# Other row counts for the split weight transfers of a fused attention and spectral-mixing kernel

## The chip, the cores and the metric

The kernel runs on one core of one Trainium2 chip. Times are device microseconds of one execution; lower is better. A profile of one execution of the kernel before, with the records of its instructions, semaphores and DMA packets, is at hand.

## The reference

Two parts follow each other. The first is attention over 8 batches, 8 heads, 576 positions and 64 channels a head. The first four heads see the last 32 positions, the other four see the positions whose distance is a multiple of 32. The second part takes the joined heads as x (8 x 576 x 512), transforms along the positions, keeps 64 modes, multiplies each mode's 512 channels by that mode's own complex 512 x 512 matrix, transforms back, adds x, and adds a rectified product with one more 512 x 512 matrix:

```python
X = np.fft.rfft(x, axis=1)
Xr, Xi = (np.real(X[:, :n_modes]), np.imag(X[:, :n_modes]))
Yr = np.einsum('bmd,mde->bme', Xr, w_r) - np.einsum('bmd,mde->bme', Xi, w_i)
Yi = np.einsum('bmd,mde->bme', Xr, w_i) + np.einsum('bmd,mde->bme', Xi, w_r)
Y[:, :n_modes] = Yr + 1j * Yi
y = np.fft.irfft(Y, n=S, axis=1)
u = x + y
return (u + np.maximum(u @ w_ch, 0.0)).astype(np.float32)
```

The matrices w_r and w_i, 64 x 512 x 512 float32 each, are by far the largest inputs: 134 MB of the 163 MB that are read.

## The kernel before, in words

The weights are streamed once, in half precision in the core's memory (the transfer converts them). A unit of the stream is a mode of one half of the 512 input channels: 128 units, in an order written out by hand in `ORDER`. Units 0 to 55 are half 1, modes 0 to 55; units 56 to 103 are half 0, modes 0 to 47; units 104 to 111 are half 1, modes 56 to 63; the rest is half 0, modes 48 to 63. Half 1 can start as soon as the strided heads are transformed, while the local heads are still being computed.

Units are fetched by `w_fetch` in pairs (two modes) or, for the pairs in `QUADS` between 13 and 53, in fours. One fetch has two transfers: the real parts go to partitions 0 to 63, the imaginary parts to partitions 64 to 127. Each partition receives, of each mode, one row of 2048 elements (8 KB read, 4096 bytes written). All of these transfers are issued by GpSimd (POOL), on one DMA queue. The last two pairs are fetched mode by mode. A fetch takes place in a ring of five pairs (`wring`); three early pairs use memory that is taken for something else later. `free_pairs` counts the pairs of the ring that the products have released: `mode_pair` (line 599) and `mode` (line 642) call `w_fetch` after the matmuls that read a pair, so each fetch waits on PE.

The table `UNEVEN` says for which units the real parts go out as several transfers of fewer rows, one behind the other, in place of one of 64 rows:

```python
if i in UNEVEN and not ri:
    a = 0
    for n in UNEVEN[i]:
        nc.gpsimd.dma_start(dst[a : a + n], rows[a : a + n])
        a += n
```

The key is the first unit of the fetch. Line 185 is the issue in this loop, line 188 that of a whole transfer, line 192 that of a single mode at the end. The bytes, the places that they are written to and the products that read them are the same however a transfer is cut; only the DMA engines that carry the rows can differ.

The order of the other work is by hand too. The strided heads of the eight batches come first (lines 262 to 394), then the local heads (lines 415 to 506), each followed by its forward transform (`dft`, line 534). From there on PE alternates between the products of the stream and the rest; a list of costs (`work`, `load`) in the third stage spreads the transposes and products with the last matrix over the fetches. Attention inputs are loaded in between by the same queue: strided ones as 64 rows and 8 rows, local ones as 128 rows. After the last products the inverse transform of the last modes, the rectified part and the output follow (lines 997 to 1122, 1141 to 1143); the output is stored by SyncE (SP).

Other transfers on the same 16 DMA engines are those of the output and constants, and the fetch of the engines' own instructions (queues 8 and 14 of the page).

Of the kernel before, what the change touches and what calls it, by code (L numbers as in the profile page):

```python
# [56 lines left out]
def kernel(  # L57
# [89 lines left out]
    SPLIT1, SPLIT0 = 56, 48  # L147
    ORDER = [(1, m) for m in range(SPLIT1)] + [(0, m) for m in range(SPLIT0)]
    ORDER += [(1, m) for m in range(SPLIT1, NM)] + [(0, m) for m in range(SPLIT0, NM)]
    UNEVEN = {64: (25, 12, 27), 84: (6, 54, 4), 94: (10, 54)}  # L150
    QUADS = {p for p in range(13, 54) if (p - 13) % 5 in (0, 2)}
    wring = pw.tile([128, 2 * NWBUF, 4, DM], F16, tag="w", bufs=1, name="wring")
    w_tiles = []
# [5 lines left out]
    def w_fetch(n=1):  # L159
        free_pairs[0] += n  # L160
        while len(w_tiles) < 2 * NM:
# [13 lines left out]
            for ri, src in enumerate((moe_w_r, moe_w_i)):  # L175
# [4 lines left out]
                if ri and not m:  # L180
                    dst, rows = dst[:, 1:nm], rows[:, 1:nm]
# [4 lines that stand above are left out]
# [1021 lines left out]
```

## Time and profile before

| | |
|---|---|
| median of 3 runs | 423.68 us (423.58 to 424.56) |
| the profiled execution's own time | 423.73 us |
| its span, first to last instruction | 421.7 us |
| granted TensorE clock, mean | 0.916 |
| busy: PE, PEld | 327.8 us, 201.8 us |
| busy: DVE, ACT, POOL | 236.9 us, 220.8 us, 112.2 us |
| moved by DMA | 91.62 MB written by 29914 packets |
| read from HBM | 162.83 MB |

The span is what the page and the trace count from; the time of an execution has 2.0 us around it. Times of a line are read from groups such as "L188 POOL DMA_DIRECT2D": a line of the kernel, the engine, the operation, what is written from what, how often, the busy time, the mean of one, and the idle time of the engine ahead of it with what ended it. In the chain of waits the last instruction is followed back to what released it. A DMA there stands from its issue to its landing.

A transfer lands when each of the 16 DMA engines has counted up its semaphore; the trace records the sixteen times, not which engine each belongs to. It also records start, length and size of every DMA packet, again without the engine.

### The profile page before, as it was taken

What the parts mean: (1) busy time and instruction counts of PE and PEld (TensorE: products, weight loads), DVE (VectorE), ACT (ScalarE), POOL (GpSimd) and SP (SyncE); (2) the same over time, 40 slices, a digit from 0 to 9 for tenths busy, and PEclk for the clock granted to TensorE, in tenths of its full rate; (3) what the DMA queues carried; (4) which work ended last, traced back from release to release, by engine and by line L of the source; (5) the groups of instructions that cost most, each with busy time, mean ns of one, the idle gap of its engine ahead of it and who ended that gap; (6) DMA issues with size and microseconds to landing.
All of it is one profiled execution on the core that took longest, in us unless ns stands there. A gap on an engine that the chain in (4) does not pass through costs nothing.

```text
span 421.7 us, 9817 instructions
## 1 busy us (share of the span) xinstructions
PE 327.8 (78%) x4156; PEld 201.8 (48%) x4156; DVE 236.9 (56%) x501; ACT 220.8 (52%) x423; POOL 112.2 (27%) x183
## 2 busy tenths in 40 slices
PE   3987878679999198888867858587569748889993
PEld 3866767564656155556534424244235423444320
DVE  3788788950364224555323627756276454665795
ACT  2687778742666157475752513532153345544693
POOL 8332333322422011212031211212112213220594
PEclk9999899956999779899995989999689988999998
DMA  8999999999999999999999999999999999999498
GB/s 149 211 211 212 214 212 213 210 212 210 215 213 213 214 214 214 214 215 214 212 214 214 213 214 214 214 213 213 213 213 215 213 214 214 213 213 182 177 380 341
DMA packets 29914, 91.62 MB, mean 217 GB/s; under 512 B 3952, under 2 KB 4720, under 8 KB 29872
## 3 DMA queue, kind: packets, MB, share of 16 engines
q0 software_dynamic: 24624, 81.28, 97.2%
q1 hardware_dynamic: 4816, 9.65, 6.2%
q8 instruction: 32, 0.52, 0.5%
q10 hardware_dynamic: 432, 0.08, 0.1%
q14 instruction: 10, 0.08, 0.0%
HBM read 162.83 MB, written 9.44 MB: 409 GB/s over the span
## 4 chain that ended last, share of the span: by engine, by line
DMA 48%; PE 27%; DVE 12%; ACT 6%; issue 4%; POOL 1%; DVEq 0%; POOLq 0%; ACTq 0%
DMA wring<-in_moe_w_i_dram 43%; PE y L599 6%; DMA wring<-in_moe_w_r_dram 4%; DVE xb L243 3%; DVE kz L285 3%; PE p L1032 2%; PE sc L534 2%; ACT X L253 2%; PE p L1052 2%; PE sc L461 1%; PE tp L415 1%; ACT PL L491 1%; PE y L534 1%; DVE rec L242 1%; DMA ring<-in_v_dram 1%
## 5 line engine op out<-in xcount | busy, mean ns | idle before, releaser
L599 PE MATMUL y<-wring,X 128*32 128x512 f16 (+1 forms) x424 | 49.1, 454 | 34.5 <-DMA wring<-in_moe_w_i_dram 34.5
L188 POOL DMA_DIRECT2D wring<-in_moe_w_r_dram x39 | 23.7, 607 | 186.4 <-PE y L599 162.5
L253 ACT ACTIVATE yr<-y 128x512 f16<-128x512 f32 x28 | 16.7, 597 | 59.7 <-PE y L599 58.0
L599 PEld LDWEIGHTS <-X 128*32 128x32 f16 (+1 forms) x448 | 21.9, 143 | 48.2 <-DMA wring<-in_moe_w_i_dram 33.0
L751 DVE COPY xo<-tp 128x512 f16<-128x512 f16 x32 | 22.1, 692 | 38.0 <-PE tp L749 38.0
L741 PE MATMUL sc<-w_cp,xT 128*128 128x512 f16 x128 | 37.4, 416 | 1.4 <-DVE xT L709 1.4
L750 ACT ACTIVATE v<-sc 128x512 f16<-128x512 f32 x32 | 19.1, 597 | 36.1 <-PE sc L741 36.1
L243 DVE TENSOR_TENSOR xb<-av,rec 90x256 f16<-90x256 f32 (+2 forms) x80 | 36.0, 450 | 2.7
L491 ACT ACTIVATE PL<-sc 128x480 f16<-128x480 f32 (+1 forms) x48 | 26.9, 578 | 17.2 <-PE sc L477 16.8
L242 DVE RECIPROCAL rec<-av 90x4 f32<-90x4 f32 (+2 forms) x80 | 14.6, 183 | 35.0 <-PE av L506 24.3
L422 DVE COPY qT<-tp 128x576 f16<-128x576 f16 x16 | 11.9, 752 | 37.3 <-PE tp L415 37.3
L1004 DVE TENSOR_TENSOR xo<-p,xo 128x512 f16<-128x512 f32 x32 | 20.6, 686 | 18.2 <-PE p L784 18.2
L188 POOL DMA_DIRECT2D wring<-in_moe_w_i_dram x42 | 25.5, 608 | 9.6 <-DMA wring<-in_moe_w_i_dram 5.3
L380 ACT ACTIVATE PL<-sc 90x360 f16<-90x360 f32 (+1 forms) x48 | 22.8, 490 | 7.0 <-PE sc L373 6.4
L253 ACT ACTIVATE v<-p 128x512 f16<-128x512 f32 x32 | 17.5, 594 | 14.9 <-PE p L784 14.8
L415 PE MATMUL tp<-cI_s,ring 64*64 64x64 f16 x864 | 23.1, 199 | 2.3 <-DVE qT L422 1.7
L253 ACT ACTIVATE v<-tp 128x640 f16<-128x640 f16 (+1 forms) x24 | 19.0, 807 | 10.6 <-PE tp L449 7.9
L461 PE MATMUL sc<-cMl_s,cI_s 128*128 128x480 f16 (+1 forms) x48 | 19.3, 403 | 5.0 <-ACT PL L491 3.4
L415 PEld LDWEIGHTS <-ring 64*64 64x64 f16 x864 | 18.3, 113 | 8.3 <-issue 4.2
L253 ACT ACTIVATE kz<-tp 64x360 f16<-64x360 f16 (+1 forms) x32 | 18.9, 592 | 6.1 <-PE tp L415 5.2
L1090 POOL TENSOR_TENSOR rl<-rl,xo 128x512 f32<-128x512 f32 x15 | 17.1, 1161 | 14.7 <-DVE rl L1083 13.0
L534 PEld LDWEIGHTS <-xb 108*128 108x128 f16 (+2 forms) x176 | 15.4, 106 | 10.8 <-DVE xb L243 6.2
(153 smaller groups left out, 763.1 us busy)
## 6 DMA issues: line engine op xcount, KB each, us to landing
wring<-in_moe_w_r_dram POOLq DMA_DIRECT2D x17, 1024.0 KB, 17.5
wring<-in_moe_w_i_dram POOLq DMA_DIRECT2D x16, 1024.0 KB, 21.8
wring<-in_moe_w_i_dram POOLq DMA_DIRECT2D x24, 512.0 KB, 17.8
wring<-in_moe_w_r_dram POOLq DMA_DIRECT2D x22, 512.0 KB, 14.7
out_dram<-osb SPq DMA_DIRECT2D x18, 256.0 KB, 2.4
out_dram<-osb SPq DMA_DIRECT2D x9, 512.0 KB, 3.3
ring<-in_v_dram POOLq DMA_DIRECT2D x8, 288.0 KB, 13.3
ring<-in_q_dram POOLq DMA_DIRECT2D x8, 288.0 KB, 13.5
```

The source lines that it names most:

```text
L188: nc.gpsimd.dma_start(dst, rows)
L243: nc.vector.tensor_tensor(out=dst, in0=val.rearrange("p h (q c) -> p h c q", c=4), in1=rec[0:n, 0:pieces] .to_broadcast((n, pieces, 64)) . ...
L253: nc.scalar.activation(out=out, in_=in_, func=ACTF.Copy)
L380: nc.scalar.activation(out=PS[0:n, ds(POFF[t], 4 * n)], in_=scp[0:n, 0 : 4 * n], func=ACTF.Exp, scale=SCALE,)
L415: nc.tensor.transpose(tp[ds(64 * hp, 64), ds(64 * i, 64)], qn[ds(64 * hp, 64), ds(64 * (9 * g + i), 64)], idn[ds(64 * hp, 64), ds(64 * hp, ...
L461: nc.tensor.matmul(scp[:, 0 : n * times].rearrange("p (h x) -> p h x", h=times), idn, mask_rows("cMl", n, times), start=True, stop=False,)
L491: nc.scalar.activation(out=dst, in_=src, func=ACTF.Exp, scale=SCALE)
L534: nc.tensor.matmul(xp[:, ds(192 * cp, 192)].rearrange("p (f m) -> p f m", f=3), xb[b][0:n, base + t, ds(128 * cp, 128)], F[0:n, :, t, :], ...
L599: nc.tensor.matmul(yp[ds(a, 32), :], Xh[half][pr, c].rearrange("p b r (h m) -> p (b r h) m", h=2)[:, :, mm % 32], wt[pr, XC[c], :], start= ...
L741: nc.tensor.matmul(vp, xT[:, ch], w_chs["cp"][:, ch, :], start=(ch == 0), stop=(ch == 3),)
L751: nc.vector.tensor_copy(out=xo.rearrange("p (h q c) -> p h q c", h=2, c=4), in_=tp[:, 0:512].rearrange("p (h c q) -> p h q c", h=2, c=4),)
L1004: nc.vector.tensor_tensor(out=xo[:, j], in0=up[j], in1=xo[:, j], op=AluOp.add)
```

## The change

Three fetches lose their cuts and four others are cut:

```diff
-    UNEVEN = {64: (25, 12, 27), 84: (6, 54, 4), 94: (10, 54)}
+    UNEVEN = {44: (20, 44), 64: (28, 36), 70: (50, 14), 86: (52, 12)}
```

Unit 44 is pair 22 (half 1, modes 44 and 45), unit 64 is pair 32 (half 0, modes 8 and 9); both are fetches of two modes. Units 70 and 86 are pairs 35 and 43, fetches of four modes, so each of their rows is twice as long in all. Unit 84 is pair 42, unit 94 pair 47; their real parts become single transfers of 64 rows. Eight pieces remain eight pieces, of four transfers in place of three. POOL issues one transfer fewer in all. No instruction of PE, DVE, ACT or SP is added, removed or moved.

## The prediction

> **What bounds the kernel now.** I read the page first, then the chain of waits, then the table of stretches for the last microseconds of the weight stream, then the trace's own records of DMA packets and landings. The page:
>
> ```profile
> span 421.7 us, 9817 instructions
> ...
> DMA  8999999999999999999999999999999999999498
> GB/s 149 211 211 212 214 212 213 210 212 210 215 213 213 214 214 214 214 215 214 212 214 214 213 214 214 214 213 213 213 213 215 213 214 214 213 213 182 177 380 341
> ...
> q0 software_dynamic: 24624, 81.28, 97.2%
> ...
> q8 instruction: 32, 0.52, 0.5%
> ...
> DMA 48%; PE 27%; DVE 12%; ACT 6%; issue 4%; POOL 1%; DVEq 0%; POOLq 0%; ACTq 0%
> ```
>
> From the second slice to the 36th the DMA engines never rest and move 210 to 215 GB/s. Sixteen engines at 213.5 GB/s write a packet of 4096 bytes each in 16 x 4096 / 213.5 = 0.307 us; in the packet records one engine's packets follow each other every 0.3045 us. So the stream of POOL's queue (q0) is a fixed amount of work, and its end can move only by how that work is shared out. The chain of waits around that end:
>
> ```profile
> 361.25 19.41 DMA wring<-in_moe_w_i_dram
> 380.66 0.28 issue
> 380.94 9.58 DMA wring<-in_moe_w_i_dram
> 390.52 0.14 issue
> 390.66 0.41 PE y L642 x8
> ```
>
> The last transfer lands at 390.52 us; PE's last mode starts 0.14 us later, and 31 us of output work follow. The stretches before it (PE, PEld, DVE, ACT, POOL busy, clock, then DMA share and GB/s):
>
> ```profile
> 384.00:385.00 1.00, 1.00 (x20) 0.69 (x19) 0.67 (x2) 0.77 (x2) 0.00 (x0) 1.00 1.07 217
> 385.00:386.00 1.00, 1.00 (x6) 0.47 (x5) 0.62 (x2) 0.54 (x2) 0.00 (x0) 1.00 1.00 197
> 386.00:387.00 1.00, 1.00 (x21) 0.65 (x21) 0.89 (x2) 0.55 (x2) 0.00 (x0) 1.00 0.91 180
> 387.00:388.00 1.00, 0.54 (x4) 0.05 (x4) 1.00 (x3) 0.60 (x1) 0.00 (x0) 1.00 0.91 180
> 388.00:389.00 1.00, 0.89 (x18) 0.68 (x19) 0.46 (x1) 0.00 (x0) 0.00 (x0) 1.00 0.68 135
> 389.00:390.00 1.00, 1.00 (x5) 0.29 (x3) 0.00 (x0) 0.00 (x0) 0.00 (x0) 1.00 0.29 57
> ```
>
> The engines do not finish together: the share falls from 1.07 to 0.29 over five microseconds. The sixteen landings of the last transfer say the same: first 385.44, last 390.52, mean 389.03. Perfect sharing would end the stream 1.49 us sooner; that is the most that any new split can gain. More than a few microseconds can be lost.
>
> **How a piece is shared out.** The page's 24624 packets tell. Data: 16256 rows of weights, 1728 of strided and 3072 of local attention inputs, 512 of w_ch, together 21568; one semaphore packet for each engine of 155 transfers is 2480. 576 are left over, 4 bytes long in the records. They are what an engine without rows gets in place of rows, if R rows go to the largest number of engines up to 16 that divides R, evenly: 25 rows to five (the other eleven get 10 each, 110), 12 to twelve (8), 27 to nine (42), 6 to six (20), 54 to nine (84, twice), 4 to four (24), 10 to ten (12), and the twelve 8-row inputs 16 each (192): 576 exactly. The Trainium skill ("DMA: Bandwidth & Descriptors", section on why a DMA increments its semaphore by 16) has this rule, and beside it an exception by which some transfers from GpSimd use rows/16, rounded up, per engine; that would leave 320 packets over, so the trace bears out the rule and not the exception. I also take it that each uneven piece starts at the engine after the last one of the piece before: with that, landing times modelled for 28 transfers from 230 to 385 us are off by 0.27 us on average, with a common start by 0.86. Call the engine where the first uneven piece starts place 0.
>
> **The change, per place.** Packets more (+) or fewer than an even share, counted from the row numbers; a row is two packets in a pair and four in a four-mode transfer. The third column is how far behind the mean of 16 each place lands the last transfer now, by the fit; braces mean that the order inside is not shown.
>
> ```
> place   old   new   lag now (us)                     difference      lag then
> 0       +2    +8    -2.03                            +6  +1.83       -0.20
> 1, 2    +6    +8    } {-1.16, -0.11, -0.10, +1.49}   +2  +0.61       see text
> 3       +6    +10   }  for places 1 to 4             +4  +1.22       see text
> 4       +6    -2    }                                -8  -2.44       see text
> 5, 6    -2    -6    } {+1.21, +1.47, +1.48}          -4  -1.22       at most +0.26
> 9       -2    -10   }  for places 5, 6, 9            -8  -2.44       about -1.0
> 7, 8    +8    +6    {+0.15, +0.38}                   -2  -0.61       at most -0.23
> 10..14  -6    -6    {-0.91, -0.27, +0.48, +0.73, +0.80}  0           at most +0.80
> 15      -6    +8    -3.60                            +14 +4.26       +0.66
> ```
>
> Why the spread exists at all: q8 fetches 32 blocks of 16 KB (0.5% of 16 x 421.7 us is 34 us, 1.05 us each), and the landing lists show these going round eight engines only, so those eight fall 1 us behind at every turn. The fit puts 5, 6 and 9 and five of 10 to 15 among them. The sixth of that group is the engine at -3.60. It is one of 13 to 15, since its third small piece of pair 42 lands 0.16 us after the second (278.02 after 277.86): too soon for two packets. I take 15: then the served engines (5, 6 and 9 to 14) and the unserved (15 to 4, and 7, 8) both come in neighbouring pairs; with 13 or 14 a pair would be broken.
>
> The four of places 1 to 4 include the engine at +1.49, one of those that end the stream. Four places are open to it. I lean to 4, and no more than lean: the eight go round in order of place, so the first fetch of the trace (same turn as the 17th, just ahead of 5) is on 13; counted from there 4 closes the first half of the sixteen, and the odd engine of a half is likelier at its border. The Trainium skill (same page, "Latency and other measured facts") calls engines 7 and 15 usually the slow ones; counted from 13, place 4 is number 7, and by that page the sum would be the one below with certainty. No row here shows an engine's number.
>
> With the slow one in place 4 it falls to 1.49 - 2.44 = -0.95. Place 3 then goes to +0.06 or +1.11, by which of three it is; 10 to 14 stay at +0.80. The last landing is 0.80 to 1.11 behind the mean, not 1.49: a gain of 0.69 or 0.38. I take 0.6, nearer the first.
>
> **The small terms.** One transfer fewer (154): about 0.02 us of semaphore packets per engine. Fillers: 192 + 24 + 40 + 8 + 24 + 120 + 8 + 48 + 16 = 480, 96 fewer, at 6 ns over 16 engines 0.04 us. POOL issues:
>
> ```profile
> L188 POOL DMA_DIRECT2D wring<-in_moe_w_r_dram x39 | 23.7, 607 | 186.4 <-PE y L599 162.5
> ```
>
> The extra issue before w_i at four places delays it and what POOL has queued behind (the next fetch and, near pair 35, the memsets of line 944) by 0.6 us; three old places give back five issues. This is hidden: POOL sits idle 186 us before this group alone, and each issue comes about 9 us ahead of its first packet (pair 22's first is issued at 168.85, and the engine furthest ahead lands it at 180.85). Without that cover it would cost 0.6 us once. Midway (250 to 294 us) places 5 and 6 run 6 packets over and the last landings come perhaps 1.6 us later than now; in exchange the 9 us spread after pair 42 goes. PE waits for weights either side and the end is set by the last transfer, so both cost nothing unless the queue runs dry, which 8 us of queued work prevent.
>
> PE must follow. Between 381 and 390 it is nearly full; before the last mode it idles 0.6 us, before the one at 388.11 another 0.57. So about 1.2 us can be taken over, then PE binds. 0.6 fits.
>
> The sum: 423.73 (the profiled execution; span 421.7, and 2 us around it) - 0.6 - 0.05 = 423.1. The median 423.68 is 0.05 lower, so 423.0 to 423.1.
>
> **Rivals.** First, the slow engine is in place 1 or 2: it lands 1.49 + 0.61 = 2.10 behind, 0.6 later than now, 424.3; in place 3, 2.71 behind, 424.9. For: the rows leave four places. Against: only the lean above.
>
> Second, and slower: the engine at -3.60 is not in place 15. Then 15 is a served engine, at -0.91 to +0.80, and +4.26 makes it the last by far: 3.35 to 5.06 behind, the stream 1.9 to 3.6 us longer, 425.6 to 427.3. It decides as soon as place 15 now lags more than 1.49 - 4.26 = -2.77. For: only 10 to 12 are excluded by a row. Against: the pairs.
>
> Third, the pieces are not laid as I say but from a fixed engine with rounded-up shares. Engines 0 to 3 would have 8 packets over now and 12 then, 4 x 0.3045 = 1.2 us more: 424.9. Against: 576 and not 320.
>
> Fourth, PE or the queue takes the gain: 423.7.
>
> **Numbers.** About 0.3% (1.27 us) is what a measurement of this kernel can tell from no change. Forecast 0.58 (423.1, own range 422.8 to 423.5); place 1 or 2 0.12, place 3 0.05; place 15 wrong 0.12; fixed start 0.02; gain lost 0.03; a better balance than counted 0.08, bounded by 1.5 us at 422.2. The range 422.2 to 424.4 leaves out place 3, place 15 and fixed start, 0.19 in all. Slower by over 0.3% (above 424.95): place 15 and part of the 424.9 cases, 0.16. Faster by over 0.3% (below 422.41) needs 85% of the whole spread: 0.06. Within: 0.78.
>
> **What will show it.** q0 should count 21568 + 154 x 16 + 480 = 24512 packets. The last weight landing should move from 390.52 to about 389.9, the share in the stretch 385:386 stay near 1.06 and fall within some two microseconds, since the first engine then lands about 1 us before the mean and not 3.6. A long tail of one engine, share near 0.07 for 2 us or more, would mean place 15 or place 3 is wrong. The same GB/s before 384 us confirms that only sharing moved; a lower one would overturn the whole reading.

## The result and the profile after

The changed kernel is slower: 425.27 us median (424.1 to 428.45, 21 runs) against 423.81 us (423.44 to 424.56, 21 runs), ratio 1.0041, 95% interval 1.0027 to 1.0056. The profiled execution took 425.27 us. The page of the changed kernel, in the lines that answer to those shown of before:

```profile
span 423.3 us, 9816 instructions
...
DMA  8999999999999999999999999999999999998498
GB/s 150 212 213 214 213 213 212 211 212 211 214 214 213 214 213 214 214 214 215 211 212 214 213 201 213 216 213 213 216 213 216 214 214 213 214 212 163 173 380 340
...
q0 software_dynamic: 24512, 81.28, 97.0%
...
q8 instruction: 32, 0.52, 0.5%
...
DMA 51%; PE 19%; issue 3%; DVE 2%; ACT 2%; POOL 1%; DVEq 0%; POOLq 0%
```

24512 packets are what the prediction counted. Two slices differ from before: the 24th (243 to 254 us) has 201 GB/s where it had 214, and the 37th, in which the stream ends, 163 where it had 182. The chain of waits around that end:

```profile
362.93 19.34 DMA wring<-in_moe_w_i_dram
382.27 0.28 issue
382.55 9.59 DMA wring<-in_moe_w_i_dram
392.14 0.14 issue
392.27 0.41 PE y L642 x8
```

The last weights land at 392.14 us, 1.62 us later than before (390.52), and PE starts 0.14 us behind them as before. What follows is unchanged: 425.27 - 392.14 = 33.13 us to the end of the execution, before 423.73 - 390.52 = 33.21. So the whole loss lies ahead of 392.14. The stretches of the changed kernel there (PE, PEld, DVE, ACT, POOL busy, clock, DMA share, GB/s):

```profile
386.00:387.00 1.00, 1.00 (x20) 0.73 (x19) 1.00 (x2) 0.37 (x1) 0.00 (x0) 1.00 1.02 201
387.00:388.00 1.00, 1.00 (x14) 0.55 (x12) 0.51 (x2) 0.93 (x2) 0.00 (x0) 1.00 0.99 197
388.00:389.00 1.00, 1.00 (x18) 0.43 (x14) 1.00 (x3) 0.18 (x2) 0.00 (x0) 1.00 0.79 156
389.00:390.00 1.00, 0.34 (x9) 0.23 (x8) 1.00 (x3) 0.57 (x1) 0.00 (x0) 1.00 0.46 90
390.00:391.00 1.00, 1.00 (x19) 0.65 (x16) 0.07 (x1) 0.00 (x0) 0.00 (x0) 1.00 0.07 12
391.00:392.00 1.00, 0.73 (x4) 0.12 (x2) 0.00 (x0) 0.00 (x0) 0.00 (x0) 1.00 0.04 8
```

A share of 0.07 and 12 GB/s is one engine out of sixteen: it works alone for the last one and a half microseconds. The sixteen landings of the last transfer have their mean at 389.59 (before 389.03), the fifteenth is 1.04 us behind the mean and the sixteenth 2.55 (before 1.48 and 1.49). So 1.62 = 0.56 + 1.06: the whole stream is 0.56 us late, and one engine is 1.06 us later against the mean than the last one was.

The 0.56 us come from the slow slice. Stretches of the changed kernel inside it:

```profile
248.00:249.00 1.00, 0.00 (x0) 0.00 (x0) 0.00 (x0) 0.00 (x0) 0.00 (x0) 0.50 1.08 213
249.00:250.00 1.00, 0.65 (x8) 0.41 (x12) 0.00 (x0) 0.00 (x0) 0.00 (x0) 0.50 1.38 164
250.00:251.00 1.00, 1.00 (x14) 0.19 (x4) 0.00 (x0) 0.00 (x0) 0.00 (x0) 0.50 0.91 127
251.00:252.00 1.00, 1.00 (x6) 0.28 (x3) 0.00 (x0) 0.60 (x1) 0.33 (x1) 0.50 1.08 217
```

From 249 to 251 us fewer bytes move, and yet the share of these two stretches together is 1.14 (elsewhere 1.07), so the engines are not idle: packets of 4096 bytes, 324 ns long as a rule, take up to 888 ns, on all engines at once. Pair 35 is being loaded then, the one cut into 50+14 rows. I call packet time beyond 324 ns, summed over the packets of q0 between 150 and 391 us, the excess: 23.3 us here, 8.7 before; a sixteenth of it is an estimate of what a mean engine loses.

The bytes that q0 has delivered say it more directly. The changed kernel is 0.02 us ahead of the kernel before at 248 us, 0.74 us behind at 255, and 0.54 us behind at 380. So the slow slice costs about 0.76 us, and 0.2 us come back between 270 and 340 us, where the kernel before loads its own cut pairs 42 and 47.

A caution for every mean below: executions differ before any cut. Up to 26 us the kernels of all runs are the same, and the profiles have delivered the same bytes there up to 0.37 us earlier or 0.33 us later than the kernel before. The lag, measured from each profile's own mean, is free of this.

### The profile page after: what moved, and what is told of

The parts are those of the page before. It is cut to its first block, busy times and chain, and to the rows that moved or that the text cites. A ratio compares the mean times of both kernels' runs of the same rounds, so it can differ in the third digit from the quotient of the medians.

```text
span 423.3 us, 9816 instructions
## 1 busy us (share of the span) xinstructions
PE 323.6 (76%) x4156; PEld 199.5 (47%) x4156; DVE 236.9 (56%) x501; ACT 220.7 (52%) x423; POOL 111.1 (26%) x182
## 3 DMA queue, kind: packets, MB, share of 16 engines
q0 software_dynamic: 24512, 81.28, 97.0%
## 4 chain that ended last, share of the span: by engine, by line
DMA 51%; PE 19%; issue 3%; DVE 2%; ACT 2%; POOL 1%; DVEq 0%; POOLq 0%
DMA wring<-in_moe_w_i_dram 43%; DMA wring<-in_moe_w_r_dram 8%; PE y L599 5%; PE p L1032 2%; PE p L1052 2%; PE sc L741 2%; PE sc L461 1%; POOL wring L188 1%; PE tp L415 1%; PE p L760 1%; ACT PL L491 1%; PE sc L477 1%; ACT X L253 1%; PE y L534 1%; PE u L1042 1%
## 5 line engine op out<-in xcount | busy, mean ns | idle before, releaser
L750 ACT ACTIVATE v<-sc 128x512 f16<-128x512 f32 x32 | 19.1, 597 | 34.6 <-PE sc L741 34.5
L415 PE MATMUL tp<-cI_s,ring 64*64 64x64 f16 x864 | 22.2, 196 | 3.3 <-DVE qT L422 2.7
L1087 ACT ACTIVATE rl<-p 128x512 f32<-128x512 f32 x35 | 18.9, 595 | 2.7 <-PE p L1052 1.2
```

What stands on the lines that cost most here:

```text
L415: nc.tensor.transpose(tp[ds(64 * hp, 64), ds(64 * i, 64)], qn[ds(64 * hp, 64), ds(64 * (9 * g + i), 64)], idn[ds(64 * hp, 64), ds(64 * hp, ...
L750: nc.scalar.activation(out=v0, in_=vp, func=ACTF.Copy)
```

## The experiments

Two theories, then. S: the late engine is a matter of shares, as the prediction's first rival has it. D: the cuts make packets slow. Every experiment changes the table of cuts and nothing else; each was timed against the kernel before on the same chip. Two readings of the trace serve throughout: the lag (last landing behind the mean of sixteen, at the last weight transfer) and the excess.

**The changed kernel again, no cuts, the cut of pair 35 moved, equal cuts.**

```diff
 c1_after  UNEVEN = {44: (20, 44), 64: (28, 36), 70: (50, 14), 86: (52, 12)}
 c2_none   UNEVEN = {}
 c3_moved  UNEVEN = {44: (20, 44), 64: (28, 36), 76: (50, 14), 86: (52, 12)}
 c4_even   UNEVEN = {44: (32, 32), 64: (32, 32), 70: (32, 32), 86: (32, 32)}
```

> The changed kernel once more, unaltered. In its first profile the last weight lands at 392.14 us against 390.52 before; the mean of the last transfer's sixteen landings is 0.56 us later (389.59 against 389.03) and the last one 2.55 instead of 1.49 us behind that mean. Theory S (sharing): the 1.06 us are the row shares, so the last landing is again 2 to 3 us behind the mean, with one engine alone at the end, and the time is about 425.3. Theory D (lost DMA time): the 0.56 us are packets that took up to 888 ns instead of 324 between 249 and 251 us; if the change causes that, it comes again at the same transfers (about 13 us of packet time lost over the engines); if it is chance, the mean is back at 389.0 and only S is left, 424.8. Theory F (fetches): the 16 KB blocks of the instruction queue begin on another one of the eight engines in each execution, so the order of the engines at the end differs from the first profile and the spread of the times (424.1 to 428.5) comes from there: the last lag would then differ by about 1 us from 2.55.

Measured 424.94 us (424.07 to 426.64; ratio 1.0029, 1.0018 to 1.0040). Last landing 391.38, mean 389.09, lag 2.29, again one engine 1.0 us behind the fifteenth. The same stretch as above, in this execution of the changed kernel:

```profile
249.00:250.00 1.00, 0.96 (x12) 0.53 (x16) 0.00 (x0) 0.00 (x0) 0.00 (x0) 0.50 1.03 205
250.00:251.00 1.00, 1.00 (x13) 0.18 (x6) 0.00 (x0) 0.00 (x0) 0.00 (x0) 0.50 1.10 221
```

No slow packets here (excess 5.8 us), and the mean is back. The instruction fetches began on another engine (their durations, 893 to 975 ns, repeat with a period of eight, and the pair of 893 comes at other numbers), yet the lag is nearly the same. So S came in both executions, D in one of the two, and F does not set the lag.

> No transfer is cut (the table is empty). By the prediction's places, taking the old shares away leaves the places at -2.64 (0), -2.99 to -0.34 (1 to 4), +1.82 to +2.09 (5, 6, 9), -2.3 to -2.1 (7, 8), +0.92 to +2.63 (10 to 14) and -1.77 (15): the last landing 2.6 us behind the mean, 1.1 us later than in the kernel before, so about 424.9, and no lone engine at the end but a group of seven or eight within 1.7 us. If the cuts cost more by themselves than they even out (theory D, or issue time), it is 423.8 or less. The count of packets should be 21568 + 150 x 16 + 192 = 24160.

Measured 424.29 us (423.85 to 424.71; 1.0011, 1.0003 to 1.0020), 24160 packets. The sixteen lags are -2.86 to -0.35 for eight engines and +1.08 to +2.42 for the other eight, close to what the prediction's places give (-2.99 to -0.34 and +0.92 to +2.63): the two kinds of engine are real. The tail of this kernel has the other shape, several engines late together, with a share of 0.46 and 0.23 in place of 0.07:

```profile
389.00:390.00 1.00, 1.00 (x19) 0.65 (x16) 0.05 (x1) 0.00 (x0) 0.00 (x0) 1.00 0.46 90
390.00:391.00 1.00, 0.73 (x4) 0.12 (x2) 0.00 (x0) 0.00 (x0) 0.00 (x0) 1.00 0.23 45
```

The time is 0.6 us below what S alone expected. Half of that is an earlier mean: 388.72 against 389.03 in the kernel before, whose excess is 8.7 us against 4.5 here. By the bytes delivered, 0.24 us of it arise after 255 us, where the old cuts lie. The old cuts, too, paid for part of their better balance with slow packets.

> The cut of 50+14 rows is moved from pair 35 to pair 38, the next four-mode transfer; row counts, places and order of the pieces stay, so every engine carries the same in the end. Theory S: last landing 2.55 us behind the mean as in the changed kernel, 425.3. Theory D, with the stretch of slow packets caused by the cut: it moves with it, to about 262 to 266 us, and the time is 425.3 too, but the place of the loss in the GB/s row shows it; if it needs what is queued just at pair 35 (two engines 2.5 us ahead of the rest), it is gone, mean 0.56 us earlier, 424.7.

Measured 425.11 us (424.16 to 426.74; 1.0034, 1.0023 to 1.0044), lag 2.70. The slow packets are there again (excess 19.4 us) and have moved with the cut. Stretches of the kernel with the cut at pair 38:

```profile
263.00:264.00 1.00, 0.76 (x10) 0.52 (x11) 0.75 (x2) 0.10 (x1) 0.00 (x0) 1.00 1.13 225
264.00:265.00 1.00, 1.00 (x8) 0.53 (x9) 0.79 (x2) 0.01 (x1) 0.00 (x0) 1.00 1.12 152
```

> The same four transfers are cut, but each into 32+32 rows, which sixteen engines share evenly: four more issues and 64 more semaphore packets than with no cut, and no engine with more rows than another. If cutting by itself costs nothing, as the prediction has it, it equals the kernel with no cut within 0.1 us (theory S: about 424.9 for both). If an issue on POOL's queue or the further semaphore packets cost something on the path, it is longer than that by 0.6 us or more.

Measured 424.65 us (424.18 to 425.65; 1.0017, 1.0009 to 1.0026): lag 2.51, excess 4.4 us, as with no cut. The median is 0.36 us above that kernel, but the intervals overlap, and in the two profiles about 0.2 us of the difference are there at 26 us, long before the first cut. Whether an equal cut costs something stays open; the 0.6 us of an issue on the path are not there.

**A map of places, and a test of it.** From the landing lists of six profiles (nine later) I fitted which place holds which engine: every list from pair 22 on is taken as row surplus x 0.3045 us, plus the fetches each served engine has had, plus one constant for each engine. The best fits miss a landing by 0.14 us on average. They leave the eight served engines where the prediction has them (5, 6, 9 to 14) and 15 unserved; but the slow one of the others is in place 3, and place 4 holds the earliest. A fit is an argument, so it was tested:

```diff
 c5_swap     UNEVEN = {44: (20, 44), 64: (36, 28), 70: (50, 14), 86: (52, 12)}
 c6_onecut   UNEVEN = {64: (25, 15, 24)}
 c7_twocuts  UNEVEN = {64: (25, 7, 32), 84: (3, 40, 21)}
```

> The changed kernel with the two pieces of pair 32 exchanged, 36+28 in place of 28+36. By the row rule this takes two packets (0.61 us) from the engines in places 3 and 4 and gives two to places 0 and 15; all others carry what they carried. Theory S3 (the lone late engine of the changed kernel sits in place 3): its lag falls from 2.3 or more to 1.7 us behind the mean, and the time from about 424.95 to 424.3. Theory S1 (it sits in place 1 or 2, which keep their rows) : the lag stays at 2.3 and the time at 424.95. If it sat in place 0 or 15: 2.9 and 425.5. Theory D (what counts is packet time lost after the skew at pair 35, not the shares): the skew there is the same, the time stays at 424.95 with a spread of 2.5 us.

Measured 424.23 us (423.6 to 426.0; 1.0013, 1.0001 to 1.0024), lag 1.85, the first engine 4.05 ahead. The tail of this kernel:

```profile
389.00:390.00 1.00, 1.00 (x14) 0.53 (x11) 0.00 (x0) 0.00 (x0) 0.00 (x0) 1.00 0.23 45
390.00:391.00 1.00, 0.54 (x3) 0.04 (x1) 0.00 (x0) 0.00 (x0) 0.00 (x0) 1.00 0.02 4
```

Two packets less for places 3 and 4 made the median 0.7 us lower than the 424.94 above (the two intervals just overlap), and the lag is 1.85 where S3 had 1.7 and S1 2.3: S3 holds; S1 and theory D alone fall. The swap tells places 3 and 4 from the others, not from each other; but place 4 carries 12 packets less than place 3 in the changed kernel and cannot be the last there. Slow packets at 249 us remain (excess 13.1 us).

> One transfer only is cut, pair 32 into 25+15+24 rows. A map of places worked out from the six profiles so far (eight engines served with instruction blocks in 5, 6 and 9 to 14; the slow one of the others in 3; 4 the fastest) gives the last landing 1.8 us behind the mean where no cut gives 2.4: 0.6 us less, 423.7. If the map is wrong in which eight are served, the 15 and 24 rows fall on engines that are late already and it is no better than no cut, 424.3 or more. 24320 packets by the row rule.

Measured 424.07 us (423.63 to 425.05; 1.0004, 0.9995 to 1.0013), lag 2.06, 24320 packets, excess 4.5 us. Better than no cut by 0.2 us where 0.6 was expected; the intervals overlap, so it speaks for the map only weakly.

> Two pairs are cut, pair 32 into 25+7+32 and pair 42 into 3+40+21 rows, chosen with the same map: last landing 1.2 to 1.35 us behind the mean (no cut 2.4), largest skew on the way 4.8 us, as at the end without cuts. Theory S: 424.3 - 1.1 = 423.2, that is 0.6 us less than the kernel before with two cuts in place of three. If every cut takes 0.3 us of DMA time by itself, 423.8. 24480 packets by the row rule.

Measured 423.76 us (423.22 to 424.68; 0.9997, 0.9989 to 1.0006), lag 1.57, excess 4.9 us. 0.5 us better than no cut, level with the kernel before. The map is 0.1 to 0.4 us short in these three. A price of 0.3 us for every cut would give 423.8 as well, and 424.0 with one cut; but by the bytes delivered these two kernels lose only 0.1 us more than no cut between 165 and 380 us, so the traces show no such price.

**Spread with equal shares.** Here later cuts give back what the first ones took, so S expects the time of no cut.

```diff
 c8_skew      UNEVEN = {70: (15, 49), 86: (63, 1)}
 c10_quadskew UNEVEN = {70: (25, 39), 76: (42, 22), 86: (20, 44)}
 c14_pairskew UNEVEN = {64: (54, 10), 74: (39, 25), 84: (44, 20), 94: (15, 49)}
```

> Two four-mode transfers are cut so that the second undoes the first: pair 35 into 15+49, pair 43 into 63+1 rows. By the row rule every engine has carried the same after pair 43, so theory S alone expects what no cut gives: last landing 2.4 us behind the mean, 424.3. Between the two, from about 250 to 295 us, six engines are 28 packets (8.5 us) behind nine others. Theory D: engines so far apart make packets slow (the profiles with 23 and 27 us of excess packet time have the excess right behind the 50+14 cut): mean of the last landings 0.5 to 3 us later than 388.7, times above 425 with a spread of more than 2 us. If instead the engines ahead run out of work, the trace shows gaps of theirs in place of long packets, and the loss would be up to 9 x 2 / 16 = 1 us.

Measured 426.13 us (425.24 to 426.61; 1.0050, 1.0038 to 1.0062), though the lag is 2.01. The mean is at 390.19, 1.47 us later than with no cut, the excess 35.1 us. Theory D, by packets and not by gaps: engines stand still mainly between 264 and 267 us, for some 2.4 us in all, 0.15 us of a mean engine.

> Three four-mode transfers (pairs 35, 38, 43) are cut so that after the third every engine has carried the same as without cuts; on the way the engines are up to 6.4 us apart. Theory S alone: as with no cut, lag 2.5 us, 424.3. Theory D, with the loss growing with the spread (12 us of spread cost 1.5 us of the mean, 5 us nothing): 0.2 to 1.0 us more, 424.5 to 425.3, packets of 400 to 900 ns between 250 and 295 us. If the loss needs a spread as large as 8 us, 424.4.

Measured 426.06 us (425.38 to 426.8; 1.0051, 1.0037 to 1.0064), lag 2.66, mean 389.73, excess 29.3 us: more than any theory expected at 6.4 us of spread. The worst of it, in the stretches of the kernel with three four-mode cuts:

```profile
261.00:262.00 1.00, 1.00 (x14) 0.68 (x12) 0.27 (x1) 0.66 (x2) 1.00 (x2) 1.00 1.04 209
262.00:263.00 1.00, 1.00 (x8) 0.50 (x6) 1.00 (x3) 0.24 (x2) 0.09 (x1) 1.00 1.40 172
263.00:264.00 1.00, 0.49 (x9) 0.39 (x8) 1.00 (x4) 0.45 (x1) 0.00 (x0) 1.00 1.03 115
```

> Spread between engines made with pairs alone, 32, 37, 42 and 47, which nearly cancel: up to 7.2 us between 250 and 300 us, lag at the end 2.65 us against 2.5 with no cut. Shares alone: 424.45. If the spread alone makes packets slow, whatever the transfer: 425.5 to 426.5, like the three four-mode cuts that made 426.06 out of 424.29. If it takes four-mode cuts (whole engines without a row for 6 us, two stretches of one transfer read at once): 424.4 to 424.8. 24640 packets by the row rule.

Measured 425.68 us (425.56 to 426.94; 1.0047, 1.0035 to 1.0059), lag 3.05, mean 389.35, excess 17.6 us. Pairs do it too; a four-mode cut is not needed.

Two more kernels were meant for this and for a better balance, and had entries without effect: units 72 and 78 are the second halves of four-mode transfers and have none of their own, so each kernel ran without them.

```diff
 c9_fivecuts  UNEVEN = {44: (18, 6, 40), 64: (6, 18, 40), 72: (5, 56, 3), 84: (7, 50, 7), 94: (28, 9, 27)}
 c11_pairskew UNEVEN = {64: (54, 10), 72: (39, 25), 78: (44, 20), 84: (15, 49)}
```

> Five pairs (22, 32, 36, 42, 47) are cut into three pieces each, chosen with the map of places (eight engines served with instruction blocks in 5, 6 and 9 to 14, the slow one in 3): last landing 0.7 us behind the mean by the map, 0.9 us with the 0.2 us by which the map has so far been short; first and last engine never more than about 4 us apart. Theory S with D (shares set the last lag, and no packets get slow at such a spread): against the kernel before, 0.6 us less lag and about 0.3 us of slow packets less, plus 0.15 us for six more transfers than its 154: 423.1 to 423.4, faster than both kernels. If each cut costs 0.3 us by itself, 424.4. 24736 packets by the row rule.

> The same kind of spread made with two-mode transfers (pairs 32, 36, 39, 42), which nearly cancel at the end: up to 7.0 us between first and last engine from about 250 to 280 us, lag at the end 2.65 us by the map against 2.5 with no cut. Theory S alone: 424.45. Theory D by the spread alone, whatever the transfer: as much more as the kernel with the four-mode cuts, 424.6 to 425.4. Theory D by the four-mode cut (rows of four modes, whole engines without rows for 6 us): 424.45, and hardly any packet over 400 ns.

Measured 424.96 us (424.25 to 426.32; 1.0025, 1.0015 to 1.0035) and 427.71 us (427.01 to 428.1; 1.0084, 1.0072 to 1.0097). What they test is the map with the cuts that took place: it gives a lag of 2.0 for the first (measured 2.56) and 5.4 for the second (measured 4.52, the largest of all). In the second, seven engines land within 0.19 us of each other at the front of the last transfer, where the first seven land over 1.64 us with no cut, and fewer bytes move well before the stream ends:

```profile
378.00:380.00 2.00, 1.44 (x12) 0.50 (x9) 2.00 (x5) 1.08 (x2) 0.40 (x1) 1.00 1.09 217
382.00:384.00 2.00, 2.00 (x26) 1.08 (x26) 1.58 (x3) 1.03 (x3) 0.52 (x1) 1.00 1.02 203
386.00:388.00 2.00, 2.00 (x25) 1.16 (x24) 1.29 (x2) 1.31 (x3) 0.00 (x0) 1.00 0.98 178
```

The last engine was 9.7 us behind the first until then: with such a spread the queue did run dry for those in front, as far as their landing together shows. A part of the fall is slow packets again (5.9 us of its 22.8 us of excess lie behind 380 us).

**What theory D can't be.** These traces narrow it: a spread that merely stands costs next to nothing. From 292 to 380 us the engines of c11_pairskew land 8.3 to 9.9 us apart, and the excess of that stretch is 2.0 us; with no cut it is 1.2. The kernel before has them 7.6 to 9.1 us apart from 284 to 309 us with 8.7 us of excess in its whole stream. In c8_skew they are 12 us apart from 257 to 264 us with an excess of 0.2, and 26.4 of its 35.1 us lie at 247 to 257 and 281 to 290 us, while its two cut transfers are loaded. So the slow packets go with unequal pieces on their way, not with the spread that these leave behind.

**The changed kernel without the cut of pair 35, and two kernels made with the map.**

```diff
 c15_no70      UNEVEN = {44: (20, 44), 64: (28, 36), 86: (52, 12)}
 c12_threecuts UNEVEN = {54: (15, 40, 9), 64: (6, 52, 6), 84: (4, 40, 20)}
 c13_fivecuts  UNEVEN = {44: (15, 40, 9), 54: (5, 56, 3), 64: (21, 40, 3), 74: (3, 40, 21), 84: (21, 40, 3)}
```

> The changed kernel without the cut of pair 35 (50+14); pairs 22, 32 and the four-mode pair 43 stay cut. By the map the last landing is 2.97 us behind the mean, against 2.31 in the changed kernel, so the shares alone make it 0.65 us slower than the changed kernel: 425.6. If the slow packets behind the 50+14 cut are half a microsecond of the changed kernel's median and more of its slowest runs, and go with the cut: 425.1, with a spread of 1 us in place of 2.5 us. 24368 packets by the row rule.

Measured 425.02 us (424.69 to 426.23; 1.0030, 1.0019 to 1.0041). The shares are worse, as expected (lag 3.62 in the profile), yet the median is that of the changed kernel: what the shares lose, the missing cut seems to give back. The times spread over 1.5 us, and the profile has slow packets at 288 to 290 us, behind the cut of pair 43 (excess 11.6 us).

> Three pairs (27, 32, 42) are cut, into 15+40+9, 6+52+6 and 4+40+20 rows, chosen with the map of places so that the last landing is 1.0 to 1.2 us behind the mean and first and last engine stay within 3.7 us of each other on the way. Shares and slow packets together expect: lag 0.3 us less than in the kernel before (1.49), slow packets 0.3 us less, 0.04 us for two more transfers: 423.2 to 423.4. If the shares decide nothing at this size, 423.85 like the kernel before or the one with two cuts (423.76). 24480 packets by the row rule.

Measured 423.80 us (423.17 to 425.38; 0.9997, 0.9987 to 1.0007): level with the kernel before. Its lag was 1.49, not 1.2. (This profiled execution ran at a granted clock of 0.806, with 34.5 us behind the last landing; its 425.38 is the longest of the twelve.)

> Five pairs (22, 27, 32, 37, 42) are cut into three pieces each; by the map the last landing is 0.7 us behind the mean and the engines stay within 2.6 us of each other from pair 27 on. Shares: 0.8 us less lag than in the kernel before and 0.3 us less of slow packets, against 0.13 us for six more transfers than its 154: 422.9 to 423.2, the fastest of all. If a cut costs 0.2 us by itself in some way not seen yet, 423.8. 24832 packets by the row rule.

Measured 423.32 us (423.01 to 424.86; 0.9992, 0.9983 to 1.0000), lag 1.03, the smallest of all. But the mean is at 390.08, the excess 39.0 us. Its row of GB/s:

```profile
GB/s 147 213 213 213 215 211 212 211 211 211 214 213 212 215 213 215 215 212 215 210 216 214 212 215 207 211 205 212 211 215 213 214 213 213 214 214 190 177 380 339
```

The slices from 253 to 306 us (25th to 29th) hold 205 to 212. In the packet records, slow stretches of one to two microseconds begin at 264, 268.5, 273.5 and 278.5 us, and the first engine lands a four-mode transfer at 265.48, 270.46, 275.38 and 280.36: one stretch in each transfer, at the same part of it, while the sixteen engines stand within 3.2 us of each other (4.3 at one piece of pair 42).

The kernel with five cuts and the one with none were then run once more, unaltered.

> The kernel with five pairs cut into three pieces each, unaltered. In its first profile the mean of the last landings was 390.08 us, 1.4 us later than with no cut, after stretches of slow packets that came back about every 4.9 us between 256 and 305 us (39 us of packet time beyond 324 ns), though the engines stood within 3 us of each other. If these stretches are tied to the cuts and come in every execution, mean and median repeat: 390.1 and 423.3 to 424.3. If they come by chance, this profile has 5 to 10 us of such time, the mean near 388.7, the last landing near 389.8, and an execution of about 423.0; the median stays near 423.3, under the kernel before by 0.4 us or more.

Measured 423.50 us (423.13 to 424.88; 0.9991, 0.9979 to 1.0003), lag 1.04, mean 389.99. The excess is 24.0 us; the series from 264 on is faint this time, but slow stretches at 257 to 259 and 282 to 284 us, at the cuts of pairs 37 and 42, are there in both profiles. The mean repeats, so these stretches are tied to the cuts. Both profiled executions are among the slower of their kernel, though: 424.36 us is the second longest of eleven, 424.19 the fourth longest of twelve. That most executions lose less to slow packets is likely, not shown.

> The kernel with no cut, unaltered. If unequal pieces are what brings the slow packets, this profile has again less than 6 us of packet time beyond 324 ns between 150 and 391 us (4.5 in the first), the last landing about 2.4 us behind the mean, and a median of 424.3 with a spread of 1 us. If slow packets come by chance in any kernel, they can show here too: 10 us or more.

Measured 424.37 us (423.94 to 425.11; 1.0009, 1.0001 to 1.0018), lag 2.50, excess 4.5 us. Three profiles without unequal pieces have 4.4 to 4.5 us, those with them 4.5 to 39.0: the slow packets belong to unequal cuts. Not every unequal cut brings them, as the 4.5 and 4.9 us of the kernels with one and two cuts show.

## Why the prediction was wrong

**The bound, and the row rule: right.** In every profile the time is the last weight landing plus 33.0 to 33.4 us (c12_threecuts apart, with its clock). Packet counts follow the row rule: 24512 as counted, 24160, 24320 and 24480 in the other kernels. PE follows.

**Place 15: right.** The engine 3.60 us ahead of the mean took 14 packets more and is not the late one. The prediction expected the first engine to be only about 1 us ahead afterwards; it is 3.70 ahead, and this is place 4: -1.16 (its group's lowest) - 2.44 = -3.60.

**The step that failed: the slow engine leaned to place 4.** It is in place 3. The prediction's own sum for that case was 1.49 + 1.22 = 2.71 behind the mean and 424.9 us, with a chance of 0.05; measured are lags of 2.55 and 2.29 in two profiles of the changed kernel (2.70 with the cut at pair 38) and medians of 425.27 and 424.94. The lone engine with a share near 0.07 was named as its sign and came. The lean rested on a guess, that the odd engine stands at the border of a half, and on a place to count from that was only assumed. By the Trainium skill ("DMA: Bandwidth & Descriptors", "Latency and other measured facts"), engines 7 and 15 are usually the slow ones; counting from the first fetch, place 3 is number 6. No run here shows an engine's number, so the runs speak against my count and not against the page; nor is "usually" the certainty that the prediction read in it. With four places open, 0.58 for place 4 beside 0.12 and 0.05 for the other three was too much, and the rows of the table gave place 3 the largest price.

**The second step: "costs nothing unless the queue runs dry".** The queue did not run dry in the changed kernel (its records never have fewer than sixteen packets in flight between 150 and 384 us), and the cuts cost DMA time all the same: 0.76 us in the slow slice of the first profile, of which 0.56 are left in the mean; in the second profile the mean is 0.06 us later. The sum put this term at nothing. A lower GB/s before 384 us, named as what would overturn the reading, came in one of the two. It overturns less than was said: the 1.06 us of lag stand beside it. The range of the changed kernel's times, 424.1 to 428.45 against 423.44 to 424.56 before, is wider than its shares explain; that these are such stretches in executions that were not traced is likely, not shown.

**The rivals.** Place 15 wrong, fixed start, and gain lost to PE did not happen. The first rival did, in its case of place 3, plus a term that no case held.

**The limit of the gain: right in size, wrong in reach.** At most 1.49 us lay in the sharing. The kernel with five cuts took 0.46 of them (lag 1.03); its medians are 0.64 and 0.53 us below the kernel before, with intervals that reach 1.0000 and 1.0003, and the means of its two profiles lie 1.1 to 1.4 us later than those of the two with no cut. It is faster than the changed kernel, and at the edge of what can be told from the one before.

## What to carry to other kernels

Where the end of a stream is set by the slowest of sixteen engines, work out for every engine what a new split gives it, and weigh each open place by its own price: a loss that one place in four decides is not a small chance. A split is also paid for on the way; read the row of GB/s slice by slice and the length of single packets, not only the last landing, and profile the changed kernel twice. The median of several runs, with no split at all as a third kernel beside old and new, says what a split is worth: here the old cuts bought 0.44 us (0.34 when measured again), not the 1.1 us that their shares promised.

## What the runs showed of the hardware that was not expected

- Packets of all engines at once became slow, 324 ns to as much as 888 ns for 4096 bytes in the changed kernel (1168 in c11_pairskew), with semaphore packets of 22 ns taking up to 158, in stretches of one to three microseconds during or after unequal cuts. The same kernel had 23.3 us of such excess in one execution and 5.8 in the next. A spread between engines that merely stands does not bring it (2.0 us of excess in 88 us at 8.3 to 9.9 us of spread), and 39.0 us came at little over 3 us of spread. What the packets wait for is not shown; the return at the same part of each transfer speaks for something in which engines meet at certain distances from each other. This was not tried further.
- The place where the first uneven piece starts looks to be the same engine in every execution: c9_fivecuts ends ten places further on than it began, and the map would give lags from 2.0 to 6.2 us if the next execution went on from there; its eleven times lie within 2.1 us, and its profile fits the start at place 0 best. The kernel with five cuts ends four places on, and its two profiles have lags of 1.03 and 1.04. The fetch of instruction blocks does move: its cycle of eight durations began at four different points in the profiles.
- A piece of one row of a four-mode transfer is not one engine's: c8_skew has 24656 packets, 48 fewer than the row rule gives, which fits if its four packets go to four engines and the other twelve get one filler each.
